# Which array form a product takes after scores, and over how many score rounds the late loads are spread

## The chip, the core and the metric

One core of one Trainium2 chip runs the whole program. The core has five engines with an instruction stream each: TensorE (PE) for matrix products, VectorE (DVE), ScalarE (ACT), GpSimd (POOL), and SyncE (SP), which here only issues transfers. They meet through semaphores. The metric is the device time of one execution in microseconds, median of several runs; lower is better.

## The reference

Two rounds of an attention layer A and a dense layer B, each with a layer norm ahead of it and a residual behind it, on x of 2048 tokens by 640 features in bf16:

```python
x = x + A(layernorm(x)); x = x + B(layernorm(x))
x = x + A(layernorm(x)); x = x + B(layernorm(x))

# A: 32 heads of 20 features, 4 segments of 512 tokens
for s in range(4):
    p      = softmax(qs @ ks.T * scale + causal mask)       # inside the segment
    a_dot  = p @ vs
    a_mem  = (phi(qs) @ M) / (phi(qs) @ z + 1e-6)           # memory of the segments before
    out_s  = g * a_mem + (1 - g) * a_dot                    # g = sigmoid(beta), per head
    M, z   = M + phi(ks).T @ vs, z + sum(phi(ks))
A = concat(out_s) @ wo
# B: relu(x @ w1) @ w2, 640 -> 1728 -> 640
```

## The kernel before

The kernel is a scheduler written in Python that runs while the program is built. Every part of the computation (scores, exponentials, value products, projections, dense layer, loads) is a stream of operations. The scheduler keeps a clock of its own for each engine, takes again and again the operation that can start first (priorities decide ties), and writes it to the end of its engine's instruction stream. What reaches the chip is five fixed streams with waits between them; nothing is decided there.

Matrix products stand in one of three forms of the PE array. Scores contract over 20 features, and four of them run side by side on different rows of the array (`rows`). Value products write 21 columns, and four of them run side by side on different columns (`cols`). All other products can be written in either of two forms: as one matmul of 128 by 128 (`full`), or as four matmuls of 128 by 32 (`cols`).

```python
def quarters(a):
    return [(slice(32 * c, 32 * c + 32), a[:, 32 * c:32 * c + 32]) for c in range(4)]

# in group(), used by all projections and the dense layer
def mm(e, dst, k=k, a=a, b=b):                     # full: profile line L673
    return e.matmul(view(dst.ap, b), a, b, start=(k == 0), stop=(k == last))
def quarter(e, dst, rows, part, k=k, b=b):         # cols: profile line L676, four of these
    return e.matmul(view(dst.ap[rows], b), part, b, start=(k == 0), stop=(k == last))
```

The form is chosen when the scheduler places the product. Outside of scores, the product takes the form that the array already has. Behind scores the kernel before looks ahead: if a value product can start within 2500 ns of the scheduler's own clock, the product takes the column form at once, otherwise the full form.

```python
def _mode(self, op):
    if op.cols is None:
        return op.mode
    if self.mode != "rows":
        return self.mode
    return "cols" if self.soon < self.free["pe"] + 2500 else "full"
```

In the update of the attention memory (L1129) the column form also does less: from the second block of tokens on, a quarter computes only the heads that lie in its 32 rows (2 or 3 heads of 21 columns: 42 or 63) instead of all 7 or 8 heads of the chunk (147 or 168).

```python
for y, (rows, part) in enumerate(quarters(phk[:, c, i, :])):
    hs = heads_of(c, y) if i else (CH_H0[c], CH_H1[c])
```

The loads that are not needed at once are 23 pieces (four of x for segment 2, five of wo, four of x for segment 3, ten of w1), and 15 more of w2. Each waits for the exponentials of one score round. A pair of head groups `m` has five rounds, so round r is (r // 5, r % 5). All are issued from SP, whose stream also issues the stores of q and k to a scratch tensor (L961), the reads of it into `pad` for the scores (L1008) and the transposing transfers (L716).

```python
pieces = x_pieces(2) + [wo rows x5] + x_pieces(3) + [w1 halves x10]     # shortened
n2 = len(pieces)                                                      # 23
pieces += [w2 rows x15]                                                # shortened
for n, (name, nbytes, fn) in enumerate(pieces):
    w = yield Need("ex", *divmod(25 + (n - n2) // 2 if n >= n2 else n * 19 // n2, 5))
    ...
    tk = yield dma("sp", sems[name], nbytes, fn, w[:1] + (w2w if n >= n2 else []) + z1, ...)
```

The second half of w1 and its rest of 64 columns wait for the last w1 piece, w2 waits for all of its pieces.

Of the kernel before, what the change touches and what calls it, by code (L numbers as in the profile page):

```python
# [38 lines left out]
class Prog:  # L39
    def __init__(self, sems):  # L40
        self.ops = {e: [] for e in ENGS}
        self.clk = dict(sems)
        self.cnt = {e: 0 for e in ["act", "dve", "pool", "pe"]}
        self.dcnt = {}
        self.K = {e: {} for e in ENGS}
        self.pos = {e: 0 for e in ENGS}
        self.info = {}
# [36 lines left out]
    def dma(self, e, fn, sem):  # L84
        self.pos[e] += 1
        self.dcnt[id(sem)] = self.dcnt.get(id(sem), 0) + 16
        tk = (sem, self.dcnt[id(sem)])
        self.ops[e].append(("op", fn, sem, 16))
        self.info[(id(sem), tk[1])] = ("dma%d" % id(sem), tk[1], dict(self.K[e]))
        return tk  # L90
# [86 lines left out]
class Sched:  # L177


    def __init__(self, prog):  # L180
        self.P = prog
        self.free = {e: 800.0 for e in ENGS}
        self.t = {}
        self.events = {}
        self.streams = []
        self.dma_free = 0.0
        self.rank = {}
        self.mode = "full"
        self.soon = 0.0
        self.landed = set()  # L190

    def add(self, prio, gen):
# [6 lines left out]
    def set(self, *key, tks=()):  # L199
        assert key not in self.events, key  # L200
        self.events[key] = [t for t in tks if t is not None]
# [39 lines left out]
    def _mode(self, op):  # L241
        if op.cols is None:
            return op.mode
        if self.mode != "rows":
            return self.mode
        return "cols" if self.soon < self.free["pe"] + 2500 else "full"

    def _alts(self, op):
        res = []
# [48 lines left out]
    def run(self):  # L298
        while True:
            best = None  # L300
            moved = True
            while moved:
                moved = False
                for st in list(self.streams):
                    had, ended = st[2], st[4]
                    self._settle(st)
                    moved = moved or st[4] != ended
                    moved = moved or st[2] is not had
            heads = []
            self.soon = min([max([self.at(t) for t in st[2].waits], default=0.0) for st in self.streams  # L310
                             if not st[4] and isinstance(st[2], Op) and st[2].mode == "cols" and st[2].cols is None],
                            default=1e12)
            for n, st in enumerate(self.streams):
                if st[4]:
                    continue
                if isinstance(st[2], Op):
                    heads.append((st[0], n, st, self._alts(st[2]), st[2], self._late(st[2])))
                elif isinstance(st[2], Either):
                    both, lone = st[2].fn()
                    if both is not None:  # L320
                        heads.append((st[0], n, st, self._alts(both), both, self._landing(both)))
                    if lone is not None:
                        heads.append((8, n, st, self._alts(lone), lone, LONE_NS))
            for prio, n, st, alts, op, late in heads:
                ok = []
                for end, start, k, e in alts:
                    if not any(p2 < min(prio, HOLDERS) and st2 is not st
                               and any(e2 == e and s2 + HOLD_TOL[e] < end for _, s2, _, e2 in al2[:1])
                               for p2, _, st2, al2, _, _ in heads):
                        ok.append((end, start, k))  # L330
                if not ok:
                    continue
                end, start, k = min(ok)
                key = (round(start + late), 0.5 if op.urgent else prio, self.rank[id(st[1])], n)
                if best is None or key < best[0]:
                    best = (key, st, end, start, k, op)
            if best is None:
                stuck = [st for st in self.streams if not st[4]]
                if not stuck:
                    return  # L340
                raise RuntimeError("stuck: " + "; ".join(
                    str(getattr(st[2], "key", None) or [s.name for s in getattr(st[2], "slots", [])][:2]) for st in stuck))
            _, st, end, start, k, op = best
            e, hold, fns, tail = op.alts[k]
            if e == "pe":
                op.mode = self._mode(op)
                self.mode = op.mode
                if op.mode == "cols" and op.cols is not None:
                    fns = op.cols
            waits, slot = op.waits, None  # L350
            for s in op.take:
                s.free = False
            if op.acq is not None:
                slot = self._pick(op.acq)
                slot.free = False
                waits = waits + slot.tks
                fns = [(lambda eng, fn=fn, slot=slot: fn(eng, slot), mark) for fn, mark in fns]
            self.P.waits(e, waits)
            self.free[e] = end
            if op.dma is not None:  # L360
                tk = self.P.dma(e, fns[0][0], op.dma)
                self.landed.add((id(tk[0]), tk[1]))
                self.dma_free = max(self.dma_free, start + 300.0) + tail[1]
                self.t[(id(tk[0]), tk[1])] = max(self.dma_free, end) + tail[0]
                if tail[2]:
                    self.free[e] = max(end, self.dma_free)
                out = tk
            else:
                marks = []
                for fn, mark in fns:  # L370
                    tk = self.P.op(e, fn, mark)
                    if tk is not None:
                        self.t[(id(tk[0]), tk[1])] = end + tail
                        marks.append(tk)
                out = marks[0] if len(marks) == 1 else (marks or None)
            st[2], st[3] = None, ((slot, out) if slot is not None else out,)
# [52 lines left out]
def bass_interleave_layers__memory_aug_infini_attn__dense_activation_relu__prompt_kernel(  # L429
    nc, A_x, A_wq, A_wk, A_wv, A_wo, A_beta, B_x, B_w1, B_w2, out,  # L430
):
    with contextlib.ExitStack() as es:
# [119 lines left out]
        def late_loads():  # L552

            def x_pieces(s):
                def one(t):
                    return lambda e: e.dma_start(x_sb[:, t, :], xs[:, t, :])
                return [("x%d" % s, 163840, one(4 * s + i)) for i in range(4)]

            def rows(name, w, src, k):
                return (name, 163840, lambda e: e.dma_start(w[:, k, :], src[128 * k:128 * k + 128, :]))  # L560

            def half(k, h):
                cs = slice(h * (DFF // 2), (h + 1) * (DFF // 2))
                return ("w1%d" % h, 221184, lambda e: e.dma_start(w1_r[:, k, cs], B_w1[128 * k:128 * k + 128, cs]))

            pieces = x_pieces(2)
            pieces += [rows("wo", wo_r, A_wo, k) for k in range(FC)]
            pieces += x_pieces(3)
            pieces += [half(k, h) for h in range(2) for k in range(FC)]
            n2 = len(pieces)  # L570
            pieces += [rows("w2", w2_r, B_w2, k) for k in range(NFULL)]
            pieces += [("w2", 81920, lambda e, z=z: e.dma_start(
                w2_r[64 * z:64 * z + DREM, NFULL + z, :], B_w2[NFULL * 128:DFF, :])) for z in range(2)]
            z1 = yield Need("z1")
            sems = {}
            left = {}
            for name, _, _ in pieces:
                left[name] = left.get(name, 0) + 1
            for n, (name, nbytes, fn) in enumerate(pieces):
                if name not in sems:  # L580
                    sems[name] = sem_("d_" + name)
                w = yield Need("ex", *divmod(25 + (n - n2) // 2 if n >= n2 else n * 19 // n2, 5))
                if n == n2:
                    v0 = yield Need("v00")
                    q1 = yield Need("q01")
                    w2w = v0 + q1 + early_done
                tk = yield dma("sp", sems[name], nbytes, fn, w[:1] + (w2w if n >= n2 else []) + z1, issue=400.0, lat=4500.0)
                left[name] -= 1
                if left[name] == 0:
                    S.set(name, tks=[tk])  # L590
# [1045 lines left out]
```

## Time and profile before

| what | before |
|---|---|
| median of 3 runs | 555.64 us (555.41 to 556.31) |
| span of the profiled execution | 553.7 us |
| PE busy | 545.7 us (99%), 8340 matmuls |
| DVE busy, ACT busy, POOL busy | 414.2, 408.7, 191.9 us |
| granted PE clock | 1.000 |
| PE share of the chain that ended last | 89% |
| exponentials (ACT, L1254) | 320 of 1026 ns |

"Busy" is the time in which at least one instruction of the engine is in flight. A matmul of 512 columns is in flight for 380 ns, while the next one starts 216 ns after it, so busy PE says that it always had something under way, and the distance between starts says what a matmul costs. In rows such as `128*32 128x512`, 128*32 is the part of the array that is used (rows by columns) and 512 is the number of columns streamed through it.

### The profile page before, as it was taken

The numbers are of one execution on the slowest core, as the hardware profiler recorded it, in microseconds if no ns is written. First come the engines' busy times: TensorE is split into PE (matmuls) and PEld (weight loads), VectorE is DVE, ScalarE is ACT, GpSimd is POOL, SyncE is SP. The second block draws the span as 40 slices with busy tenths as digits, with TensorE's granted clock in tenths as the row PEclk, the third lists the DMA queues.
The fourth block names the chain that finished last, engine by engine and source line by source line (L and its number), as shares of the span: only waits on it lengthen the run. The fifth ranks groups of instructions, "written<-read, shape, count | busy, mean of one in ns | idle before, by whom it ended". The sixth has DMA issues, their size and how long they took to land.

```text
span 553.7 us, 19086 instructions
## 1 busy us (share of the span) xinstructions
PE 545.7 (99%) x8340; PEld 308.3 (56%) x8340; DVE 414.2 (75%) x1059; ACT 408.7 (74%) x518; POOL 191.9 (35%) x302
## 2 busy tenths in 40 slices
PE   8999999999999999999999999999999999999998
PEld 7464554455564555646446555565456654657756
DVE  5967989897898988997687998669886886417202
ACT  5699889889877888687887887778874878651140
POOL 5245344343444334343433443034430433301000
DMA  8595999933854138466276332971439322342201
GB/s 271 134 232 158 227 186 211 239 72 45 191 112 91 32 58 199 79 93 92 60 188 107 60 69 21 207 147 22 67 48 223 92 36 54 69 81 28 74 2 51
DMA packets 130292, 61.32 MB, mean 111 GB/s; under 512 B 109090, under 2 KB 120098, under 8 KB 130210
## 3 DMA queue, kind: packets, MB, share of 16 engines
q1 hardware_dynamic: 129648, 59.58, 50.8%
q8 instruction: 65, 1.06, 0.8%
q10 hardware_dynamic: 562, 0.53, 0.3%
q14 instruction: 17, 0.14, 0.1%
HBM read 20.57 MB, written 12.85 MB: 60 GB/s over the span
## 4 chain that ended last, share of the span: by engine, by line
PE 89%; DVE 5%; DMA 2%; ACT 2%; POOL 0%; SPq 0%; issue 0%; ACTq 0%; POOLq 0%
PE ps L673 42%; PE ps L676 27%; PE ps L1192 8%; PE ps L1286 6%; ACT PT L1254 2%; PE ps L1325 1%; PE ps L1072 1%; PE ps L650 1%; DMA oT<-o_sb 1%; DMA otk<-otu 1%; PE ps L1466 1%; PE ps L1129 1%; DVE hT L1490 1%; DVE xn_tok L740 1%; DMA beta_bc<-in_A_beta_dram 1%; DVE o_sb L1380 1%
## 5 line engine op out<-in xcount | busy, mean ns | idle before, releaser
L1254 ACT ACTIVATE PT<-ps 128x1024 bf16<-128x1024 f32 x320 | 309.0, 1026 | 58.6 <-PE ps L1192 57.3
L1266 POOL TENSOR_SCALAR_AFFINE_SELECT PT<-PT 128x512 bf16<-128x512 bf16 x256 | 166.6, 669 | 266.8 <-ACT PT L1254 266.7
L673 PE MATMUL ps<-w_r,hT 128*128 128x320 bf16 x488 | 78.5, 300 | 0.0
L1512 DVE TENSOR_TENSOR x_sb<-x_sb,ps 128x320 bf16<-128x320 bf16 (+1 forms) x65 | 31.1, 479 | 48.1 <-PE ps L676 34.1
L676 PE MATMUL ps<-xnT,w_r 128*32 128x512 bf16 x1092 | 64.8, 379 | 0.1
L1192 PE MATMUL ps<-pad 20*128 20x512 bf16 (+3 forms) x1024 | 63.4, 301 | 1.2 <-ACT PT L1254 1.0
L673 PE MATMUL ps<-xnT,w_r 128*128 128x512 bf16 x247 | 60.9, 380 | 0.0
L673 PEld LDWEIGHTS ps<-w_r,hT 128*128 128x128 bf16 x488 | 45.6, 98 | 23.5 <-issue 6.4
L694 DVE BATCH_NORM_STATS2 stats<-x_sb 128x6 f32<-128x320 bf16 x124 | 56.0, 474 | 2.6 <-DMA x_sb<-in_A_x_dram 2.2
L676 PE MATMUL ps<-w_r,hT 128*32 128x320 bf16 (+1 forms) x1428 | 52.4, 294 | 0.0
L1192 PEld LDWEIGHTS ps<-pad 20*128 20x128 bf16 x1024 | 17.8, 92 | 52.2 <-ACT PT L1254 28.1
L1491 ACT ACTIVATE hT<-ps 128x512 bf16<-128x512 f32 x51 | 30.5, 598 | 20.5 <-PE ps L676 19.6
L676 PEld LDWEIGHTS ps<-w_r,hT 128*32 128x32 bf16 x1428 | 37.0, 97 | 10.2
L676 PEld LDWEIGHTS ps<-xnT,w_r 128*32 128x32 bf16 x1092 | 28.3, 97 | 24.6 <-issue 0.5
L1296 DVE CAST otu<-ps 128x512 bf16<-128x512 f32 x50 | 34.2, 684 | 8.7 <-PE ps L1286 8.2
L1490 DVE TENSOR_SCALAR hT<-ps 128x512 bf16<-128x512 f32 x53 | 36.1, 682 | 6.1 <-PE ps L673 4.6
L1408 DVE TENSOR_TENSOR x_sb<-x_sb,ps 128x320 bf16<-128x320 bf16 x64 | 29.6, 477 | 14.7 <-PE ps L676 7.3
L1286 PE MATMUL ps<-PT,v_aug 128*21 128x128 bf16 (+3 forms) x896 | 40.4, 301 | 0.0
L1037 ACT ACTIVATE stg<-stg 128x512 bf16<-128x512 bf16 x50 | 31.6, 635 | 8.5 <-DVE rtmp L1035 8.5
L673 PE MATMUL ps<-wo_r,oT 128*128 128x320 bf16 x234 | 37.0, 300 | 0.3 <-DMA oT<-o_sb 0.3
L710 POOL TENSOR_TENSOR rstd<-lnU,mhalf 128x2 f32<-128x2 f32 (+2 forms) x26 | 20.3, 780 | 47.5 <-DVE lnU L706 37.6
L673 PEld LDWEIGHTS ps<-xnT,w_r 128*128 128x128 bf16 x247 | 22.2, 97 | 25.3 <-issue 3.7
(109 smaller groups left out, 737.2 us busy)
## 6 DMA issues: line engine op xcount, KB each, us to landing
pad<-scr SPq DMA_DIRECT2D x124, 80.0 KB
scr<-stg SPq DMA_DIRECT2D x34, 256.0 KB, 2.9
out_dram<-x_sb SPq DMA_DIRECT2D x15, 160.0 KB, 2.2
w_r<-in_B_w_dram SPq DMA_DIRECT2D x10, 216.0 KB, 2.5
w_r<-in_B_w_dram SPq DMA_DIRECT2D x13, 160.0 KB, 3.0
x_sb<-in_A_x_dram SPq DMA_DIRECT2D x10, 160.0 KB, 3.4
scr<-w_r SPq DMA_DIRECT2D x5, 256.0 KB, 2.9
wv_r<-in_A_wv_dram SPq DMA_DIRECT2D x1, 800.0 KB, 8.8
```

Source lines behind the costliest of these rows:

```text
L673: return e.matmul(view(dst.ap, b), a, b, start=(k == 0), stop=(k == last))
L676: return e.matmul(view(dst.ap[rows], b), part, b, start=(k == 0), stop=(k == last))
L694: tk = yield dve(320, 1, lambda e, c2=c2: e.bn_stats(stats6[:, t % 12, c2, :], x_sb[:, t, c2 * 320:(c2 + 1) * 320]), xt)
L1037: te = yield act(512, lambda e, q=q: e.activation(q, q, ACT.Exp), [tr] + p, psum=False)
L1192: fns.append([(lambda e, z=z, j=j, hh=hh, N=N, o=o, sl=sl, q=hh % 2: e.matmul(slot.ap[:, q, o:o + N], sl.ap[32 * hh:32 * hh + DH, z, 0, 12 ...
L1254: tx = yield act(1024, lambda e, dst=dst, src=src: e.activation(dst, src, ACT.Exp, scale=SCALE), sc + pw)
L1266: tm = yield pool(600.0, lambda e, reg=reg: e.affine_select(out=reg, in_=reg, pattern=[[0, 4], [1, 128]], compare_op=ALU.is_ge, fill=0.0, ...
L1286: fns.append((lambda e, OD, j=j, hh=hh: e.matmul(OD.ap[32 * hh:32 * hh + DH + 1, 128 * j:L], VAUG[vx(a, s)][:, j, 4 * g + hh, :], pt.ap[:, ...
L1296: te = yield evac(L, 1, lambda e: e.tensor_copy(dst, OD.ap), lambda e: e.activation(dst, OD.ap, ACT.Copy), [tk] + OTU[0].tks)
L1490: th = yield evac(512, 1, lambda e: e.tensor_scalar(hT[:, dc, :], bk.ap[:, :], 0.0, None, ALU.max), lambda e: e.activation(hT[:, dc, :], b ...
L1491: lambda e: e.activation(hT[:, dc, :], bk.ap[:, :], ACT.Relu), [tk] + HT.tks)
L1512: ta = yield dve(n, 1, lambda e: e.tensor_tensor(x_sb[:, t, c0:c0 + n], x_sb[:, t, c0:c0 + n], bk.ap[:, 0:n], ALU.add), [tk], urgent=True)
```

## The change

Two things are altered. The look-ahead behind scores goes: a product that follows scores now always takes the full form. And the 23 late pieces wait for rounds 0 to 22, one each, where they waited for rounds 0 to 18. The first part leaves the scheduler with the simpler rule, the second is for keeping the transfers of the first segments further apart in time. As the scheduler builds one list from everything, both also alter the order of everything placed later.

```diff
-        self.soon = 0.0
...
         if op.cols is None:
             return op.mode
-        if self.mode != "rows":
-            return self.mode
-        return "cols" if self.soon < self.free["pe"] + 2500 else "full"
+        return self.mode if self.mode != "rows" else "full"
...
-            self.soon = min([max([self.at(t) for t in st[2].waits], default=0.0) for st in self.streams
-                             if not st[4] and isinstance(st[2], Op) and st[2].mode == "cols" and st[2].cols is None],
-                            default=1e12)
...
-                w = yield Need("ex", *divmod(25 + (n - n2) // 2 if n >= n2 else n * 19 // n2, 5))
+                w = yield Need("ex", *divmod(25 + (n - n2) // 2 if n >= n2 else n * 23 // n2, 5))
```

## The prediction, made before the result was known

> **What bounds the kernel now.** I read four views in this order: the page's busy times, the busy time by stage, the waits of PE in the late stages, and the timeline of PE. The page's first part:
>
> ```profile
> PE 545.7 (99%) x8340; PEld 308.3 (56%) x8340; DVE 414.2 (75%) x1059; ACT 408.7 (74%) x518; POOL 191.9 (35%) x302
> ```
>
> PE is never idle for long, so the question is where its few idle microseconds lie. The view by stage gives for each stretch its length and then PE's busy time:
>
> ```profile
> 0.00:91.00 91.00, 86.31 (x1062) 50.43 (x1066) 72.54 (x200) 74.90 (x104) 40.64 (x73) 1.00 0.83 200
> 91.00:200.00 109.00, 108.57 (x1541) 57.03 (x1529) 95.46 (x237) 93.92 (x116) 44.06 (x66) 1.00 0.55 120
> 200.00:340.00 140.00, 139.51 (x1825) 74.66 (x1821) 119.44 (x303) 115.33 (x138) 58.88 (x90) 1.00 0.50 96
> 340.00:480.00 140.00, 140.00 (x2185) 78.28 (x2186) 104.05 (x268) 105.56 (x131) 45.05 (x69) 1.00 0.47 94
> 480.00:553.70 73.70, 71.32 (x1746) 47.89 (x1745) 22.68 (x55) 18.98 (x32) 3.27 (x5) 1.00 0.22 47
> ```
>
> Length less busy: 4.7 us idle before 91 us, 0.4 and 0.5 us in the next two stretches, none in the fourth, and 2.4 us in the last, which is the residual sum and the store after the last matmul. The waits of PE from 91 us on are only these:
>
> ```profile
> PE ps L673 <- DMA oT<-o_sb: 0.3, 1, 0.3
> PE ps L1192 <- ACT PT L1254: 0.2, 1, 0.2
> ```
>
> So from 91 us on the time is the sum of what the matmuls cost, and no transfer or other engine sets it. What they cost is read from starts in the timeline (start, time in flight, line, shape, count):
>
> ```profile
> 79.53 0.33 PE L1129 MATMUL ps<-w_r,phk 128*32 128x42 bf16 x24
> 79.69 1.25 PE L676 MATMUL ps<-hT,wk_r 128*32 128x512 bf16 x20
> ...
> 95.01 2.55 PE L673 MATMUL ps<-xnT,w_r 128*128 128x512 bf16 x11
> 97.49 0.40 PE L1192 MATMUL ps<-pad 20*128 20x384 bf16 x8
> ...
> 98.71 1.68 PE L676 MATMUL ps<-xnT,w_r 128*32 128x512 bf16 x28
> 100.33 0.40 PE L1192 MATMUL ps<-pad 20*128 20x256 bf16 x8
> ...
> 128.72 0.97 PE L1129 MATMUL ps<-v_aug,phk 128*128 128x147 bf16 x12
> 129.53 0.30 PE L673 MATMUL ps<-wv_r,xnT 128*128 128x320 bf16 x1
> ```
>
> Full form: 11 products of 512 columns and the step to scores take 97.49 - 95.01 = 2.48 us. Column form: 28 quarters, that is 7 products, and the step to scores take 1.62 us. With 0.216 us for a product in either form, 11 x 0.216 = 2.38 and 7 x 0.216 = 1.51, and 0.10 to 0.11 us is left in both for the step to the other form of the array. Products of 320 columns come out at 0.136 us in both forms in the same way. **The column form gains nothing in an ordinary product; a step between forms costs about 0.10 us.** In the memory update the forms differ: 12 full matmuls in 0.81 us are 67 ns each, 24 thin quarters, that is 6 steps, in 0.16 us are 27 ns each.
>
> **What the Trainium skill says.** "TensorE: Matmul & The Clock Gate", section "Back-to-back issue gap", gives about N/2.4 + 2.5 ns between matmuls of N columns: 216 and 136 ns for 512 and 320, as measured here. The same section gives 131 ns for N = 512 in a real stream; this trace doesn't show that. Its Part 3, "The mechanism", lets quarters on different columns start some 4 ns apart and run together, so four quarters should cost about one full matmul: the 1.62 us above agrees. "TensorEngine Tiling (Array Packing)", section "Key Properties", says that "Mode switching requires drain"; here that is the 0.10 us. "DMA: Bandwidth & Descriptors", section "Rules for kernel authors", advises to issue a transfer early and wait for it late; the late loads do so, with the margins worked out below.
>
> **The change part by part.** I laid the order of PE's instructions in both programs side by side and counted.
>
> *Products.* Of 320 columns there are 1009 full and 513 in columns before, 982 and 540 after: 1522 both times. Of 512 columns, 504 and 396 before, 530 and 370 after: 900 both times. Both forms cost the same, so this is 0. Although the rule that made columns is gone, about as many products stand in columns as before, because after a value product the form stays until the next scores.
>
> *Steps between forms.* Here I had expected the loss: without look-ahead, scores, products and a value product need two steps, with it one. The lists say otherwise. Before, scores are followed by columns 41 times, of which 34 are value products and 7 are products that the look-ahead set in columns. After it is 39 times, 38 of them value products: the scheduler now more often puts the value product straight behind the scores. Steps from full to columns number 16 in both. All steps together: 337 before, 337 after, so 0. (The look-ahead could save at most 7 x 0.10 = 0.7 us.)
>
> *Memory update.* Before there are 58 full matmuls and 62 steps in columns, of which 48 are thin. After there are 86 full and 34 in columns, of which 27 are thin. So 21 steps become wide, at 67 - 27 = 40 ns: **+0.84 us**.
>
> *First 91 us.* The first 1071 entries of PE's list (its first 1070 matmuls) are the same in both programs, up to the value product that ends at about 91.4 us; the lists of DVE, ACT and POOL agree as far as their 197th, 109th and 113th instruction, which is about the same stretch. So the 4.7 us of idle time there stay, unless a transfer moves them. They are not waits for late loads: the largest, 0.9 us, is a wait for VectorE's copy of a product, and VectorE is held up by its own queue and the power on GpSimd.
>
> *Late loads.* The pieces of x, wo and the first half of w1 move by one to three rounds, 2 to 8 us, and are needed much later: wo lands by 41 us and PE first uses it near 71 us. The last three pieces of w1 move more. Before, the last w1 load is issued here:
>
> ```profile
> 60.73 0.45 SPq L564 DMA_DIRECT2D w_r<-in_B_w_dram  x1
> ...
> 77.50 5.01 SPq L716 DMA_TRANSPOSE xnT<-xn_tok  x2
> ```
>
> After, three w1 loads stand behind those two transposes and one store to scratch (0.7 us), so they go out at about 83.3 us and land by some 87.5 (10 of the w1 loads take 2.5 us from issue to landing by the page, those behind others up to 3.6). The first product that needs them stands at about 92: hidden, but with a margin of 4 us where it was 27. For w2 the last two loads now stand behind four more reads into `pad` (1.6 us); I estimate landing at 112 us and first use, by PE's own list, 1.8 us later than the 113.05 of before. Margin about 3 us, as before.
>
> **Sum:** 0 + 0 + 0.84 + 0 = +0.84 us on 555.64, 556.5; I add 0.1 us for small new waits.
>
> **The rivals.** *A: the new order waits more.* From 91 us on almost all is a new order, and the old one had 0.9 us of idle time there up to 480 us. That speaks for a scheduler that keeps its margins, but each new order can meet a late exponential or transpose. In the old order the longest case was the oT transpose, for which the first wo product waited some 0.5 us with 16.6 us of PE work (counted from the list with the costs above) between the segment's last value product and itself. In the new order that distance is 13.1 to 15.5 us in segments 1 to 5. If two or three of them wait for 1 us, the time becomes 558 to 559. *B: the early transfers get in each other's way less,* and the waits before 91 us shrink. For it: the DMA share there is 0.83, far above the later stretches. Against it: the waits there are for DVE, ACT and GpSimd. At the most it would give back 1 us: 555.5. *C: w1 or w2 arrives late.* If my margins of 3 to 4 us were wrong by twice that, PE would stand for some 3 us: 559 to 560. *D: the new order packs better.* It can save only the 0.9 us of idle time and perhaps 1 us of small hidden waits, which leaves 554.7.
>
> **Range and chances.** The gain is bounded: work and steps are counted, 4.7 us lie in an unchanged stretch, 2.4 us at the end. So the low end is 554.6. The upper end is rivals A and C: 559.2. To be 2% faster the kernel would have to lose 11.1 us, more than all its idle time; to be 2% slower it would need 11 us of new waits.
>
> **What the new profile would show.** If the steps are right: starts of products still 216 and 136 ns apart in both forms; PE idle for 4 to 5 us before 91 us and for about 2.4 us at the end; in between up to about 2 us. A wait of PE or of its weight loads for w_r from DRAM would show C; longer waits on oT or on the exponentials A; a smaller idle time before 91 us B. I am wrong if the number of matmuls in the same forms costs a different time, or if the idle time between 91 and 480 us exceeds 4 us.

## The result, and the profile after

The changed kernel takes **560.39 us** (median of 4 runs, 559.68 to 561.64), the kernel before 555.97 us in the same measurements: ratio 1.0079, 95% interval 1.0055 to 1.0104. That is 4.4 us slower, where 1.0 us was forecast (556.6 against 555.64) and 559.2 us was the upper end of the range.

PE's busy time by stage in the changed kernel (length, then PE busy):

```profile
0.00:91.00 91.00, 85.31 (x1058) 49.02 (x1062) 72.17 (x198) 74.67 (x104) 40.70 (x73) 1.00 0.83 196
91.00:200.00 109.00, 106.92 (x1440) 55.60 (x1432) 94.11 (x236) 92.39 (x114) 42.48 (x64) 1.00 0.57 123
200.00:340.00 140.00, 139.21 (x1845) 75.05 (x1838) 120.74 (x304) 114.58 (x137) 58.74 (x90) 1.00 0.48 95
340.00:480.00 140.00, 139.63 (x2091) 77.69 (x2092) 109.73 (x278) 103.05 (x125) 47.72 (x73) 1.00 0.48 94
480.00:557.70 77.70, 74.70 (x1838) 50.38 (x1834) 23.40 (x56) 18.83 (x31) 3.19 (x5) 1.00 0.21 47
```

Between 91 and 480 us PE is idle for 2.08 + 0.79 + 0.37 = 3.24 us, where it was 0.9 before: **2.3 us of new waits in the stretch with the new order**. Before 91 us the idle time is 1.0 us longer, but that is no loss: the 52 warm-up matmuls took 4.4 us in this execution and 5.6 us in that of before, so PE waits instead for the layer norm, and the same product that stood at 89.13 us (a score round) stands at 89.28. At the end the last store lands later: idle 3.0 us, not 2.4. That need not be part of the change: over all profiles of this study the program ends 2.6 to 2.7 us after the start of its last matmul in seven, and 3.1 to 3.3 us after it in seven, and the changed kernel and run 5, whose instructions there are the same, fell on different sides. The three profiles with the lists of before are all on the short side, so this is not settled. What remains of the 4.0 us between the two profiles is the memory update, 0.8 us by the count and 0.7 us by the starts in the two traces, and small hidden waits.

PE's own waits from 91 to 480 us (waiting instruction, what released it, total, times, longest):

```profile
PE ps L1186 <- ACT PT L1248: 0.8, 2, 0.6
PE ps L667 <- DMA oT<-o_sb: 0.8, 1, 0.8
PE ps L1460 <- issue: 0.6, 1, 0.6
PE ps L667 <- DVE hT L1484: 0.4, 1, 0.4
PE ps L1186 <- DMA pad<-scr: 0.3, 1, 0.3
```

Five kinds where there were two (L1186 are the scores, L667 full products, L1460 the rest of w1). They don't have one cause: an exponential, two transfers, an operation of VectorE (hT), and one that is put down to "issue". The timeline tells what that one is. These are SP's transfers just ahead of it in the changed kernel (start, time to issue):

```profile
83.44 1.47 SPq L558 DMA_DIRECT2D w_r<-in_B_w_dram  x3
84.95 1.23 SPq L710 DMA_TRANSPOSE phk<-phs  x1
86.23 2.81 SPq L710 DMA_TRANSPOSE otk<-otu  x1
89.08 1.41 SPq L710 DMA_TRANSPOSE xnT<-xn_tok  x1
```

and the same two transposes in the kernel before:

```profile
85.99 1.82 SPq L716 DMA_TRANSPOSE otk<-otu  x1
...
87.85 1.44 SPq L716 DMA_TRANSPOSE xnT<-xn_tok  x1
```

The w1 loads land in time: issued from 83.4 us, the last in by 89.2, needed at 92. But the otk transpose behind them takes 1.0 us longer to issue, and the xnT transpose goes out 1.2 us later. It lands 3.5 us after its issue in both kernels, so at 91.3 us before and at 92.6 us after. These are the first w1 products of the two kernels:

```profile
91.42 0.61 PE L676 MATMUL ps<-xnT,w_r 128*32 128x512 bf16 x8
```

```profile
92.66 0.73 PE L1460 MATMUL ps<-xnT,w_r 128*32 128x256 bf16 x20 [0.56 <-issue]
```

In both it starts 0.09 us after xnT has landed, and so it does in nine of the fourteen profiles of this study. So already in the kernel before this product stood right behind its transpose, without a margin, although the waits of PE don't list it there. This profile alone does not show that the loads are to blame: run 1 below has a wait of 0.6 us at the same product without any loads ahead. Runs 4 and 10 test it.

### The profile page after: what moved, and what is told of

The parts are those of the page before. It is cut to its first block, busy times and chain, and to the rows that moved or that the text cites. A ratio compares the mean times of both kernels' runs of the same rounds, so it can differ in the third digit from the quotient of the medians.

```text
span 557.7 us, 18907 instructions
## 1 busy us (share of the span) xinstructions
PE 545.8 (98%) x8250; PEld 307.7 (55%) x8250; DVE 420.2 (75%) x1069; ACT 403.5 (72%) x508; POOL 192.8 (35%) x302
## 4 chain that ended last, share of the span: by engine, by line
PE 85%; DVE 6%; DMA 4%; ACT 3%; SPq 1%; issue 1%; POOL 0%
PE ps L667 41%; PE ps L670 25%; PE ps L1186 8%; PE ps L1280 6%; ACT PT L1248 2%; PE ps L1066 1%; DMA pad<-scr 1%; PE ps L1123 1%; PE ps L1319 1%; DMA oT<-o_sb 1%; PE ps L1460 1%; DMA otk<-otu 1%; DVE o_sb L1374 1%; DVE stats L688 1%; DMA beta_bc<-in_A_beta_dram 1%
## 5 line engine op out<-in xcount | busy, mean ns | idle before, releaser
L667 PE MATMUL ps<-w_r,hT 128*128 128x320 bf16 x477 | 77.4, 300 | 0.0
L1186 PE MATMUL ps<-pad 20*128 20x512 bf16 (+3 forms) x1024 | 63.4, 301 | 2.4 <-ACT PT L1248 1.6
L667 PE MATMUL ps<-xnT,w_r 128*128 128x512 bf16 x262 | 64.1, 380 | 0.5 <-DVE hT L1484 0.4
L670 PE MATMUL ps<-xnT,w_r 128*32 128x512 bf16 x1032 | 61.4, 379 | 0.0
L667 PEld LDWEIGHTS ps<-w_r,hT 128*128 128x128 bf16 x477 | 43.9, 98 | 22.6 <-issue 6.1
L670 PE MATMUL ps<-w_r,hT 128*32 128x320 bf16 (+1 forms) x1472 | 54.2, 294 | 0.0
L1186 PEld LDWEIGHTS ps<-pad 20*128 20x128 bf16 x1024 | 17.9, 92 | 54.5 <-ACT PT L1248 27.7
L1485 ACT ACTIVATE hT<-ps 128x512 bf16<-128x512 f32 x53 | 31.7, 599 | 22.4 <-PE ps L670 20.0
L670 PEld LDWEIGHTS ps<-w_r,hT 128*32 128x32 bf16 x1472 | 38.4, 97 | 10.0
L1290 DVE CAST otu<-ps 128x512 bf16<-128x512 f32 x52 | 35.5, 684 | 10.6 <-PE ps L1280 10.5
L1484 DVE TENSOR_SCALAR hT<-ps 128x512 bf16<-128x512 f32 x51 | 34.8, 682 | 5.4 <-PE ps L667 3.2
L670 PEld LDWEIGHTS ps<-xnT,w_r 128*32 128x32 bf16 x1032 | 26.6, 97 | 22.0
L667 PEld LDWEIGHTS ps<-xnT,w_r 128*128 128x128 bf16 x262 | 23.3, 97 | 27.9 <-issue 4.8
L667 PE MATMUL ps<-wo_r,oT 128*128 128x320 bf16 x213 | 33.6, 300 | 0.8 <-DMA oT<-o_sb 0.8
```

Of the source, the lines that this page charges most:

```text
L1186: fns.append([(lambda e, z=z, j=j, hh=hh, N=N, o=o, sl=sl, q=hh % 2: e.matmul(slot.ap[:, q, o:o + N], sl.ap[32 * hh:32 * hh + DH, z, 0, 12 ...
L1290: te = yield evac(L, 1, lambda e: e.tensor_copy(dst, OD.ap), lambda e: e.activation(dst, OD.ap, ACT.Copy), [tk] + OTU[0].tks)
L1484: th = yield evac(512, 1, lambda e: e.tensor_scalar(hT[:, dc, :], bk.ap[:, :], 0.0, None, ALU.max), lambda e: e.activation(hT[:, dc, :], b ...
L1485: lambda e: e.activation(hT[:, dc, :], bk.ap[:, :], ACT.Relu), [tk] + HT.tks)
```

## Experiments

In what follows "lists" means the instruction lists of PE, VectorE, ScalarE and GpSimd. Ratios are to the kernel before on the same chip, whose median was 556.2 to 556.6 us in these runs; that of the changed kernel is from the measurement above. Run 1 is e1, and so on.

### 1 and 2: each half of the change alone

```diff
# e1: from the changed kernel
-    n * 23 // n2
+    n * 19 // n2
# e2: from the kernel before
-    n * 19 // n2
+    n * 23 // n2
```

> The look-ahead is removed, the late loads keep their 19 rounds. PE's list has 336 steps between forms (before 337) and a memory update 0.4 us dearer. If removing the look-ahead is what costs the 4.4 us, this run stands at 559 to 561. If the loads cost it, at 556 to 557. If it is the luck of each new order, anything between 555 and 560, and its idle time of PE between 91 and 480 us explains its distance from before.

Measured 555.57 us, ratio **0.9989** (0.9980 to 0.9998). PE's idle time from 91 to 480 us is 0.9 us, as in the kernel before.

> The look-ahead stays, the late loads take 23 rounds. 333 steps between forms (0.4 us less than before), memory update about 0.4 us dearer. If the loads cost the 4.4 us, 559 to 561. If the look-ahead does, about 556. If each new order is its own draw, anything between 555 and 560; the stop at the first w1 product (near 92 us), which the three w1 loads between transposes are thought to cause, should then be here too, since its order of transfers there is that of the changed kernel.

Measured 559.53 us, ratio **1.0062** (1.0046 to 1.0078). The stop at the first w1 product is here too, 1.0 us long. So the look-ahead is not what was lost: without it the kernel is as fast as with it, or 0.1% faster (the rule and its new lists are not told apart in that). The loss comes with the 23 rounds, under either rule. But 23 rounds change two things, where the loads stand in SP's list and the lists of everything placed later.

### 3 and 4: only the last three w1 loads moved, all lists kept

```diff
+ late = the last three w1 loads, taken out of SP's finished list
# e3, in the changed kernel
+ put back directly behind the seventh w1 load
# e4, in the kernel before
+ put back behind the two xnT transposes and the store to scratch (as in the changed kernel)
```

> The kernel before with every engine's order kept, but for the last three w1 loads, which now go out where the changed kernel issues them, behind two transposes and a store near 83 us. If the loads hold up the transposes, a stop of 0.5 to 1 us at the first w1 product appears: 556.5 to 557. If they started a chain of delays, 558 or more. If harmless, 556.0.

Measured 557.53 us, ratio **1.0026** (1.0012 to 1.0039): 1.4 us for three loads that nobody waits for (the last landed at 89.7 us). The lists are those of before, so the two traces can be compared matmul by matmul: 1.4 us arise in one place, the first w1 product.

```profile
86.49 3.07 SPq L723 DMA_TRANSPOSE otk<-otu  x1
89.60 1.41 SPq L723 DMA_TRANSPOSE xnT<-xn_tok  x1
```

```profile
93.18 0.62 PE L683 MATMUL ps<-xnT,w_r 128*32 128x512 bf16 x8 [1.43 <-issue]
```

The transposes go out late, and the product follows xnT's landing at 93.1 us.

> The changed kernel with every engine's order kept, but for the last three w1 loads, which go out directly behind the w1 loads before them (near 61 us, not 83). If these loads hold up the transposes behind them, the 0.6 us stop at the first w1 product goes and the otk transpose is issued in 1.8 us, not 2.8: 559.5 to 560. If they started a chain of delays, 557 to 558. If they are harmless, 560.4.

Measured 561.62 us, ratio 1.0098 (1.0084 to 1.0111): **slower**, against all I expected. The wait for xnT is gone, but the loads now go out at 61 to 63 us, ahead of reads into pad, and scores wait for those:

```profile
70.62 0.40 PE L1197 MATMUL ps<-pad 20*128 20x512 bf16 x4 [2.77 <-DMA pad<-scr]
```

Moving a load out of the way of one transfer put it in the way of another. So the prediction's reading that no transfer sets the time holds only while the transfers stand where they stood.

### 5 and 6: the lists and the place of the loads, crossed

The 23 late loads were lifted out of SP's finished list and set in, with their waits, where the other kernel has them. The SP lists without these loads agree for their first 68 transfers, which covers the loads' places.

```diff
# e5: lists of the changed kernel, loads at the places and rounds of 19
# e6: lists of e1, loads at the places and rounds of 23
+ for each late load n: wait for round n * R // 23, then the load, at its place among SP's other transfers
```

> The instruction lists of PE, VectorE, ScalarE and GpSimd are those of the changed kernel. In SP's list the 23 late loads stand where the kernel with 19 rounds has them (the same place in both kernels with 19 rounds) and wait for its rounds. If the loads' place makes the loss by itself, 555.5 to 557. If the new order of everything else makes it, 559 to 560.5. If both, about 558.

Measured 558.61 us, ratio **1.0040** (1.0027 to 1.0054).

> The mirror: PE, VectorE, ScalarE and GpSimd have the lists of the kernel without look-ahead and with 19 rounds (555.6 us), the 23 late loads stand in SP's list where the changed kernel has them and wait for its rounds. If the loads' place makes the loss, 559 to 560.5. If it costs only what moving three w1 loads cost in the order of before (1.4 us), 556.5 to 557. If nothing, 555.6.

Measured 557.28 us, ratio **1.0007** (0.9993 to 1.0022).

| ratio to before | loads at 19's places | loads at 23's places |
|---|---|---|
| lists of 19 rounds, no look-ahead | 0.9989 | 1.0007 |
| lists of 23 rounds (changed kernel) | 1.0040 | 1.0079 |

Read down, the new lists cost 0.51% with the loads where they were: 2.8 us (0.72% with the loads at 23's places). Read across, the loads' new places cost 0.18% in the old lists and 0.39% in the new: 1.0 and 2.2 us. (The intervals are some 0.15% wide to each side, more for the changed kernel, so that these two differ is not shown. Those of 0.9989 and 1.0007 touch, so the 1.0 us is at the edge too; run 4, whose interval leaves out 1, is the clearer evidence that places cost.) Both theories hold in part, and the lists are the larger part.

In run 6 the places cost at two points of the profile. The first w1 product waits 0.3 us longer than in e1, and before it scores wait for a read into pad, which was in time in e1:

```profile
69.16 0.39 PE L1193 MATMUL ps<-pad 20*128 20x512 bf16 x4 [0.89 <-DMA pad<-scr]
```

Two w1 loads stand ahead of these reads where e1 has one; the changed kernel has two as well, without this wait.

In some executions the granted clock fell for a while (last section). Without these, run 4 stands at 1.0018, run 5 at 1.0032, run 6 at 1.0001 and e1 at 0.9989: the lists keep a cost of 0.4%, the places in the old lists 0.1%. So part of what the places cost comes with the falls of the clock.

The waits of PE from 91 to 480 us with the new lists and the old loads:

```profile
PE ps L1193 <- ACT PT L1255: 1.1, 3, 0.6
PE ps L1193 <- DMA pad<-scr: 1.0, 1, 1.0
PE ps L674 <- DMA oT<-o_sb: 0.4, 1, 0.4
PE ps L677 <- DMA oT<-o_sb: 0.2, 1, 0.2
```

and with the old lists and the old loads (e1):

```profile
PE ps L670 <- issue: 0.6, 1, 0.6
PE ps L1186 <- ACT PT L1248: 0.2, 1, 0.2
```

These sum to 2.7 us against 0.8. The longest wait of scores for an exponential comes with the lists and repeats in all four profiles that use them: here in the changed kernel and in e5, and the same 0.65 in e3 and e9.

```profile
264.14 0.40 PE L1186 MATMUL ps<-pad 20*128 20x512 bf16 x4 [0.65 <-ACT PT L1248]
```

```profile
262.40 0.40 PE L1193 MATMUL ps<-pad 20*128 20x512 bf16 x4 [0.65 <-ACT PT L1255]
```

The scheduler put too little PE work between two score rounds there. Waits for transfers differ between profiles with the same lists: that for pad near 368 us was 0.3 us in the changed kernel and 1.0 in e5 and in e3.

### 7, 8, 11 and 12: other numbers of rounds, all scheduled anew

One edit each, in the changed kernel: `n * 23 // n2` becomes `n * R // n2`.

> No look-ahead, late loads over 15 rounds, so all early transfers are closer together. If later loads cost time steadily, 555.6 or a little less. If each order is a draw, 555 to 561. If closer transfers hold up the reads into pad as in the run with w1 moved forward, a wait of scores for pad before 91 us appears and 557 to 559.

> No look-ahead, late loads over 21 rounds, everything scheduled anew. If later loads cost time steadily, between the 555.6 of 19 rounds and the 560.4 of 23: 557 to 559. If each new order is a draw of its own, anywhere between 555 and 561, and its waits after 91 us lie at other places than those of 23 rounds.

> No look-ahead, late loads over 22 rounds: a PE list unlike that of 19 to 21 and of 23 rounds. If the loss belongs to late loads, close to 23 rounds: ratio 1.005 to 1.008. If each list is a draw, 0.998 to 1.008, with its waits after 100 us at places of its own.

> No look-ahead, late loads over 27 rounds: the last w1 loads wait for round 25 (near 83 us). If later loads cost time steadily, more than 23 rounds: ratio above 1.008, with a wait for w1 itself of 1 us or more near 92 us. If each list is a draw, 0.998 to 1.010.

| rounds (no look-ahead) | us | ratio | 95% interval | lists |
|---|---|---|---|---|
| 15 | 558.81 | 1.0038 | 1.0023 to 1.0053 | own |
| 19 (e1) | 555.57 | 0.9989 | 0.9980 to 0.9998 | A |
| 21 | 556.48 | 0.9982 | 0.9969 to 0.9995 | A |
| 22 | 558.11 | 1.0026 | 1.0011 to 1.0042 | own |
| 23 (changed) | 560.39 | 1.0079 | 1.0055 to 1.0104 | own |
| 27 | 562.17 | 1.0096 | 1.0064 to 1.0127 | own |

With 21 rounds the lists turn out to be those of 19, only SP's list differs, and the time is the same within the intervals: later loads by themselves cost nothing up to there. Where the lists change, so does the time, in both directions of the number of rounds: 15, with loads closest together, loses 2 us, with scores waiting 1.4 us for an exponential near 117 us and no wait for pad before 91 us. So it is no steady price per round, though from 22 on all are slower (22 rounds by 0.3%, where a price of late loads asked for 0.5 to 0.8). With 27 rounds the first w1 product waits longest. The expectation had named a wait for w1 itself, but the last w1 load had landed at 90.2 us; the otk transpose behind the loads took 4.1 us to issue, and xnT landed at 93.7. The wait brings a second cost (timeline of PE; then busy times by stage, the column behind POOL is the granted PE clock):

```profile
93.76 3.30 PE L667 MATMUL ps<-xnT,w_r 128*128 128x512 bf16 x8 [1.97 <-issue]
```

```profile
94.00:98.00 4.00, 4.00 (x15) 1.15 (x14) 1.23 (x3) 1.49 (x3) 1.22 (x2) 0.57 0.99 226
```

Eight products take 3.3 us from start to end where 216 ns each would be 1.9.

The versions of 19 and 21 rounds without look-ahead are faster than the changed kernel, and by their intervals also than the kernel before, by 0.11% and 0.18%; the medians of 21 rounds and of before on that chip, 556.48 and 556.55 us, don't show the latter.

### 9: one wait of the new lists taken away

This run is e5 with one edit: three reads into pad that stood behind four transposes near 357 us go out ahead of them.

> As the run with the new order and the old loads (ratio 1.0040 to before), and three reads into pad, which stand in SP's list behind four transposes near 357 us, go out ahead of them. If the wait of scores for pad near 368 us (1.1 us in that run's profile) is made by SP's order, it is gone and the time is 1 us lower, ratio near 1.002, unless the transposes that are pushed back by 1 us make oT late instead, which the profile would show as a longer wait of the wo product near 366 us.

Measured 559.20 us, ratio 1.0045 (1.0032 to 1.0058). In the profile the wait for pad is gone, and that for oT near 366 us too, and PE regains 1.1 us on e5 there; yet the ratio is no lower than e5's 1.0040. Executions in which the clock fell don't explain it (without them 1.0049, and 1.0032 in e5). Removing this wait is not worth what its length promised; the profile is a single execution and doesn't show what took its place in the others. That stays open.

### 10: is it the issuing or the bytes?

```diff
# the kernel before, all loads at their old places; behind the store to scratch near 83 us:
+ for k in range(3): dma(junk[:, k, :], w1 rows of chunk k, columns 0:4)     # 8 bytes per partition
```

> The kernel before, all loads at their old places, with three more loads behind the store to scratch near 83 us, where the changed kernel has its last w1 loads; each brings only 4 columns of w1 (8 bytes per partition, 1 KB in all) into a tile that nobody reads. If the issuing of three loads ahead of the transposes is what made the wait of 1.6 us at the first w1 product, it is here too (ratio near 1.0026 as with the real loads). If their 216 KB each in flight did it, ratio 1.000 and a wait of 0.2 to 0.8 us there.

Measured 556.46 us, ratio 1.0002 (0.9984 to 1.0019). The three small loads take as long to issue as the real ones (1.42 us against 1.45). In the profile they hold the transposes up less: xnT goes out at 88.8 us, where it was 87.9 in the kernel before, 88.4 in e1 and 89.6 in e4, and the wait at the first w1 product is

```profile
92.37 0.61 PE L676 MATMUL ps<-xnT,w_r 128*32 128x512 bf16 x8 [0.52 <-issue]
```

against 0.6 us in e1, without any loads there, and 1.4 in e4. So the 216 KB that each real load has in flight seem to matter more than the three places in the list. The phk transpose right behind the small loads was slow to issue (2.2 us, where the changed kernel had 1.2), but so it was in e1 and e9, which have no loads there (2.3 and 2.1). The phk and otk transposes together took 2.9 to 3.6 us to issue in the five profiles of this order without a load ahead of them, 3.5 behind the three small loads, and 4.0 to 5.3 in the five with three real ones. Still, the interval of this run overlaps that of e4 (1.0012 to 1.0039), so I take it as likely, not as shown.

## Why the prediction was wrong, point by point

- **Products, steps, memory update: right.** The counts hold in the changed kernel. One part of the memory update that took 0.29 us in columns takes 0.52 in full form; over the whole kernel the starts of these groups to the next instruction add up to 7.3 us against 6.6, so 0.7 us where 0.84 was counted.
- **The look-ahead is worth nothing: right.** Run 1 shows it, ratio 0.9989.
- **First 91 us unchanged: right,** to 0.15 us. (The largest wait there is not the 0.9 us for VectorE but the 1.6 us for GpSimd at the very start, in both kernels.) Runs 3 and 6 show that this stretch is not safe from transfers: other places of the loads made scores wait for pad there.
- **Late loads, 0 us: wrong.** I worked out when the loads go out, and that was right (I said 83.3 us; they went out from 83.4). The last landed at 89.2 us, not by 87.5, so the margin to 92 was 3 us and not 4, but still a margin. The step that failed is the one after it: "hidden, but with a margin of 4 us", and so worth 0. I asked who waits for the loads and not who stands behind them, and I read from the list of waits that no transfer sets the time, while the first w1 product stood 0.09 us behind the landing of xnT. The loads' places cost 2.2 us in the new lists (1.0 in the old, at the edge of what the runs can tell; runs 5, 6 and the table), and moving three loads alone cost 1.4 us (run 4). My rival C, a wait for w1 or w2 themselves, did not happen in the changed kernel.
- **Small new waits, 0.1 us: mis-sized.** The lists of the changed kernel cost 0.51% or 2.8 us more than those of run 1 with the loads at the same places; about 0.5 us of that is its dearer memory update and steps between forms (counted as before, 0.36 and 0.11 us), the rest waits: the two profiles show 2.0 us of it as idle time of PE between 91 and 480 us (2.9 against 0.9). The term should have been some 2.3 us. That was my rival A. In the changed kernel this idle time is 3.2 us, above the 2 us that I expected and below the 4 us that I had named as a sign of being wrong. I had seen that the distance from the last value product to the first wo product shrank to 13 to 15.5 us, and the wait for oT near 142 us (0.8 us idle) is one of those. But I took 0.9 us of idle time in one good list as the measure for any list, and three other lists here (15, 22 and 27 rounds) are slower than before as well.
- **The sum.** From before to the changed kernel: -0.6 us without look-ahead (run 1), +2.8 for the new lists (run 5 against run 1), +2.2 for the loads' places in them (changed kernel against run 5), together the 4.4 us measured.
- **Rivals B and D:** not seen in the changed kernel. The lists of 19 and 21 rounds without look-ahead do pack a little better than those of before, by 0.1 to 0.2%; that stays within my low end of 554.6.

## What to carry to other kernels

When a transfer moves, check not only that it lands before its use, but what is queued or in flight behind it: a hidden load can still delay the transpose that follows. A view of waits does not show how close the others are: compare when a transfer lands with when its reader starts. And where a static scheduler places everything, a small edit draws a new list: here two lists differed by 0.5% with nearly the same work, so a blind forecast needs a term for the waits of a new list, sized from several lists, and a variant should be judged by crossing the lists with the edit itself.

## What the runs showed of the hardware that I had not expected

- After a stop of PE the granted clock fell in some executions: 0.57 on average over 4 us in the lines above (27 rounds, after 2.0 us of idle time). In the profile of run 9 it fell after a stop of 0.9 us near 56 us (0.57 from 56 to 60 us), and so it did in those of runs 2 and 7 (0.58 and 0.64 in the same stretch), while the same stop left it at 1.00 in the other eleven profiles, and a stop of 2.8 us in run 3 left it at 1.00 too. So the length of the stop alone does not decide it. Products then stand some 427 ns apart and not 216, which adds 1.5 to 1.6 us to the stop in runs 7, 9 and 12.
- Of 142 executions of the kernel before, measured beside runs 1 to 12, 16 have a mean granted clock below 1.000. They took 1.5 to 2.7 us longer than the others (medians on three chips). In runs 4 and 6 it is 5 of 22 and 4 of 14 executions.
- Behind three loads of 216 KB two transposes on SP together took 4.0 to 5.3 us to issue, and 2.9 to 3.6 without them (phk and otk near 86 us, five profiles each). Over all 86 transposes of the kernel before, the issue of one takes 1.2 to 2.6 us.
- The time from the start of the last matmul to the end of the program lay near 2.6 or near 3.2 us. With the lists of the changed kernel both occur: 2.6 in run 5, and 3.3, 3.2 and 3.1 in the changed kernel and runs 3 and 9.
